# Scores and P times V tied in pairs in TensorE's order, from the ninth step of attention on

## The chip, the cores and the metric

The kernel runs on one core of a Trainium2 chip. The metric is the device time of one execution in microseconds, as a median of several runs.

## The reference

Attention over 2 batches, 8 heads, 768 positions and head size 64, with a local window of 96 positions, 8 global positions and a distance bias; then two feed-forward blocks on the 1536 resulting rows of 512.

```
scores = q @ k.T / sqrt(64) - slope[h] * dist     # masked to local or global positions
a      = softmax(scores)
x      = a @ v                                     # as 1536 rows x 512
h = x @ w_in;  x = (h * sigmoid(h)) @ w_out        # 512 -> 2048 -> 512
out = (sigmoid(x @ w_gate) * (x @ w_val)) @ w_out2 # 512 -> 1536 -> 512
```

## The kernel before

Attention works in units. A unit n is one block of 128 positions (`gi = n // 4`, 12 blocks over both batches) and one pair of heads (`p = n % 4`); there are 48. A unit goes through these stations: `emit_T` transposes the block's K and Q of two heads on TensorE into one PSUM bank (L339), and ScalarE or VectorE copies them out (L352, L350); `emit_QK` makes the scores against at most two blocks of keys (L376), with 64 contraction rows for each of the two heads; `soft` adds the mask, takes the maximum and later the exponent and the norm (VectorE L391, ScalarE L398, VectorE L404 and L405, GpSimd L407); `emit_PT` transposes the probabilities (L424), ScalarE copies them out to one of three `pt` buffers (L428); `emit_PV` multiplies with V (L445), 64 output columns for each head. After the fourth unit of a block, `take` copies the block's result to X and starts V loads on SyncE's queue (L462, L463). The scores of units n and n+1 go to two halves of the same two banks, one bank for each head of a pair.

A step of attention handles two units, n and n+1. Its first part, `head(n)`, emits P times V of n-4 and n-3, then scores of n and n+1, `take`, and both `soft`; then follow the transposes of probabilities of n-2 and n-1 and the transposes of K and Q of n+2 and n+3. The first six steps run alone (`run_att`). The steps from n = 12 on run in `window`, which mixes their parts with the first feed-forward block's matmuls for finished groups of 512 rows (L493: 512 columns, or 256 in the first items of `PLAN`). After the window `phase_rest` does the remaining feed-forward work. Weights are fetched and split into two parts by VectorE and ScalarE (L153 to L167) as the program goes on.

All instructions are emitted in one program order. A planner then makes each engine's own order from it: on each engine, what is ready goes first by program order, so that instructions that are neighbours in the program can end up far apart. On the chip each engine runs through its order as it stands.

Of the kernel before, what the change touches and what calls it, by code (L numbers as in the profile page):

```python
# [22 lines left out]
)  # L23
HA = 8
NEG = 1.0e30
LIMIT = 1.0e8
MAX_LOCAL = 121.0
# [4 lines left out]
def attn_moe_moe2_kernel(  # L32
# [88 lines left out]

    halves1 = [range(0, HA), range(HA, C1)]
    halves2 = [range(0, C2 // 2), range(C2 // 2, C2)]
# [131 lines left out]
    def make_mask0():  # L255
# [13 lines left out]
        nc.vector.tensor_tensor(gl, gl, loc[:, gs], ALU.add)  # L269
        nc.vector.tensor_scalar(gl, gl, -1.0, NEG, op0=ALU.add, op1=ALU.mult)  # L270
        nc.vector.tensor_scalar(loc, loc, -1.0, NEG, op0=ALU.add, op1=ALU.mult)
        nc.vector.tensor_tensor(m, m, loc, ALU.add)
# [4 lines left out]
    def make_mask1():  # L277
# [14 lines left out]
        nc.gpsimd.tensor_tensor(loc[:, gs], loc[:, gs], gl, ALU.add)  # L292
        nc.gpsimd.tensor_scalar(loc, loc, -1.0, NEG, op0=ALU.add, op1=ALU.mult)
        nc.gpsimd.tensor_tensor(m, m, loc, ALU.add)
# [36 lines left out]
    def emit_T(n):  # L331
        gi, p = divmod(n, NP)
        if gi >= NBLK:
            return
        s = gi % 2
        src = qk_t[gi]
        ps = bk["T"][n % len(bk["T"])]
        for j in range(2):
            nc.tensor.transpose(  # L339
                ps[:, j * 128:(j + 1) * 128],  # L340
                src[:, j, 2 * p:2 * p + 2, :].rearrange("p h d -> p (h d)"),
                ident,
            )

        def evac():
            sc = 2.0 ** (p - 1)
            dst = kT[p][:, slice(0, 3, 2) if s == 0 else slice(1, 3), :]
            pv = ps[:, 0:256].rearrange("p (a b) -> p a b", a=2)
            if n % 2:
                nc.vector.tensor_scalar(dst, pv, sc, None, op0=ALU.mult)  # L350
            else:
                nc.scalar.activation(out=dst, in_=pv, func=AF.Copy, scale=sc)  # L352
            i = gi % BLK
            if i == 0:
                nc.gpsimd.tensor_copy(kg[p], kT[p][:, s, 0:N_GLOB])
            elif i >= 2:
                nc.gpsimd.tensor_copy(kT[p][:, 1 - s, 0:N_GLOB], kg[p])

        evac()
        if p == NP - 1:  # L360
            load_qk(gi + 2)

    def emit_QK(n):
        gi, p = divmod(n, NP)
        if gi >= NBLK:
            return
        s, i = gi % 2, gi % BLK
        kt = kT[p]
        u, m = n % 2, n // 2
        sp = [bk["SA"][m % len(bk["SA"])], bk["SB"][m % len(bk["SB"])]]  # L370
        w = 128 if i == 0 else 256
        sp = [x[:, u * 256:u * 256 + w] for x in sp]
        for e in range(2):
            r = slice(64 * e, 64 * e + 64)
            rhs = kt[r, s, :] if i == 0 else kt[r, 0:2, :].rearrange("p a b -> p (a b)")
            nc.tensor.matmul(sp[e], kt[r, 2, :], rhs, start=True, stop=True)  # L376
        return sp

    def soft(n, sp):
        if sp is None:  # L380
            return
        gi, p = divmod(n, NP)
        s, i = gi % 2, gi % BLK
        w = 128 if i == 0 else 256
        t = t_p.tile([128, 2, 256], F32, tag="t", name="t")
        t_t[n] = t
        c = 2.0 ** -(2 * p + 1)
        m0 = 0 if i == 0 else (128 if s == 0 else 256)
        ss = ssum[n % 4]
        for e in range(2):  # L390
            nc.vector.tensor_tensor_reduce(  # L391
                t[:, e, 0:w], sp[e], mask[e][:, m0:m0 + w], op0=ALU.add, op1=ALU.min,
                scale=-c, scalar=3.0e38, accum_out=nm_all[:, gi, 2 * p + e:2 * p + e + 1],
            )

        def exps():
            for e in range(2):
                nc.scalar.activation(  # L398
                    out=t[:, e, 0:w], in_=t[:, e, 0:w], func=AF.Exp, scale=-1.0,
                    bias=nm_all[:, gi, 2 * p + e:2 * p + e + 1], accum_out=ss[:, e:e + 1],  # L400
                )

        def norm():
            nc.vector.tensor_scalar(ss, ss, 1.0e-9, None, op0=ALU.add)  # L404
            nc.vector.reciprocal(ss, ss)  # L405
            for e in range(2):
                nc.gpsimd.tensor_scalar(  # L407
                    t[:, e, 0:w], t[:, e, 0:w], ss[:, e:e + 1], 1.0, op0=ALU.mult, op1=ALU.mult
                )

        defer(1 + n % 2, exps)
        defer(2 + n % 2, norm)

    def emit_PT(n):
        gi, p = divmod(n, NP)
        if n < 0 or gi >= NBLK:
            return
        i = gi % BLK
        nk = 1 if i == 0 else 2
        t = t_t.pop(n)  # L420
        ps = bk["PT"][n % len(bk["PT"])]
        for e in range(2):
            for c in range(nk):
                nc.tensor.transpose(  # L424
                    ps[:, (e * nk + c) * 128:(e * nk + c + 1) * 128], t[:, e, c * 128:(c + 1) * 128], ident
                )
        pt = pt_p.tile([128, 512], F32, tag="pt", name="pt")
        nc.scalar.activation(out=pt[:, 0:256 * nk], in_=ps[:, 0:256 * nk], func=AF.Copy)  # L428
        pt_t[n] = pt

    def emit_PV(n):
        gi, p = divmod(n, NP)
        if n < 0 or gi >= NBLK:
            return
        s, i = gi % 2, gi % BLK
        pt = pt_t.pop(n)
        ps = bk["PV"][gi % len(bk["PV"])]
        if i == 0:
            vs = [v_t[gi]]
        else:  # L440
            vs = [v_t[gi], v_t[gi - 1]] if s == 0 else [v_t[gi - 1], v_t[gi]]
        nk = len(vs)
        for c in range(nk):
            for e in range(2):
                nc.tensor.matmul(  # L445
                    ps[64 * e:64 * e + 64, p * 128:(p + 1) * 128],
                    vs[c][:, (2 * p + e) * D:(2 * p + e + 1) * D],
                    pt[:, (e * nk + c) * 128:(e * nk + c + 1) * 128],
                    start=(c == 0),
                    stop=(c == nk - 1),  # L450
                )

    def take(n):
        gi, p = divmod(n, NP)
        if n < 0 or gi >= NBLK or p < NP - 1:
            return
        i = gi % BLK
        ps = bk["PV"][gi % len(bk["PV"])]
        g, j = divmod(gi, BPG)
        xs = slice(j * 128, (j + 1) * 128)  # L460
        pv = ps.rearrange("p (a b) -> p a b", a=NP)
        nc.scalar.activation(out=X[g][:, 0, :, xs], in_=pv, func=AF.Copy)  # L462
        nc.vector.tensor_tensor(X[g][:, 1, :, xs], pv, X[g][:, 0, :, xs].bitcast(F32), ALU.subtract)  # L463
        if 0 < i < BLK - 1:
            nc.sync.dma_start(
                out=v_t[gi][0:N_GLOB, :].rearrange("p (h d) -> p h d", h=H),
                in_=v[gi // BLK, :, 0:N_GLOB, :].rearrange("h p d -> p h d"),
            )
        load_v(gi + 2)

    def att_units(m0, m1):
        def head(n):
            emit_PV(n - 4)
            emit_PV(n - 3)
            sp = [emit_QK(n), emit_QK(n + 1)]
            take(n - 3)
            soft(n, sp[0])
            soft(n + 1, sp[1])

        for m in range(m0, m1):  # L480
            n = 2 * m
            yield lambda n=n: head(n)
            yield lambda n=n: emit_PT(n - 2)
            yield lambda n=n: emit_T(n + 2)
            yield lambda n=n: emit_PT(n - 1)
            yield lambda n=n: emit_T(n + 3)
# [463 lines left out]
```

## Time and profile before

| | |
|---|---|
| median of 3 runs | 699.97 us (698.42 to 701.34) |
| the profiled execution | 700.66 us |
| its span | 698.9 us |
| TensorE busy | 683.5 us, 98% of the span |
| VectorE, ScalarE, GpSimd busy | 374.4, 278.7, 88.8 us |
| granted TensorE clock, mean | 0.99 |

The span is the time from the first to the last instruction that the profiler saw; the execution's own time has a little around it. Times in the rows are microseconds from the start of the span unless marked ns. A busy TensorE is not TensorE at its peak: consecutive matmuls overlap in the rows, so the distance from start to start tells what a stretch of matmuls costs.

### The profile page before, as it was taken

Reading aid. Unit: us, or ns where it says so; the run is one execution under the profiler, and the core shown is the slowest. Engines: PE = TensorE matmul, PEld = TensorE weight load, DVE = VectorE, ACT = ScalarE, POOL = GpSimd, SP = SyncE. Lnnn points to the kernel's source line nnn. Section 1 sums busy time; section 2 is a strip of 40 time slices with the busy share of each in tenths; the row PEclk is TensorE's granted clock in tenths of the full one; section 3 lists DMA queues with packets and bytes.
Section 4 is the critical chain, followed back from the end, with each engine's and each line's share of the span. In section 5 each row is a group of like instructions: output and inputs, shape, how many; then the busy total and the mean of one; then the engine's idle time right before and its main releaser. Section 6 shows DMA issues by size and latency. Waiting matters only on the chain.

```text
span 698.9 us, 9181 instructions
## 1 busy us (share of the span) xinstructions
PE 683.5 (98%) x3393; PEld 534.9 (77%) x3393; DVE 374.4 (54%) x861; ACT 278.7 (40%) x594; POOL 88.8 (13%) x174
## 2 busy tenths in 40 slices
PE   7899999999999999999999999999999999999995
PEld 4467886667777888888888888888888888888884
DVE  4699995544459999752389941311684211212212
ACT  3688865464446565432265521111352111111110
POOL 5355553333320000000000000000000000000000
PEclk9799999999999999999999999999999999999999
DMA  9466562120002554500025420000240000100101
GB/s 210 127 163 157 165 194 61 31 48 16 17 2 83 163 177 124 177 1 0 1 79 159 153 91 1 1 0 1 60 151 0 1 1 0 61 0 1 61 0 65
DMA packets 65300, 49.03 MB, mean 70 GB/s; under 512 B 39648, under 2 KB 60128, under 8 KB 65248
## 3 DMA queue, kind: packets, MB, share of 16 engines
q1 hardware_dynamic: 64032, 48.11, 24.0%
q8 instruction: 28, 0.46, 0.3%
q10 hardware_dynamic: 1216, 0.26, 0.2%
q14 instruction: 24, 0.20, 0.1%
HBM read 45.22 MB, written 3.15 MB: 69 GB/s over the span
## 4 chain that ended last, share of the span: by engine, by line
PE 92%; DVE 5%; ACT 1%; issue 1%; DMA 1%; POOL 0%; DVEq 0%; ACTq 0%; POOLq 0%
PE bank L493 54%; PE bank L672 14%; PE bank L670 13%; PE bank L376 4%; PE bank L445 3%; PE bank L424 3%; PE bank L339 1%; DVE t L391 1%; DMA nraw<-in_n_local_dram 1%; ACT t L398 1%; DVE w L167 1%; DVE u L158 0%; DVE u L155 0%; POOL t L407 0%; DVE u L154 0%
## 5 line engine op out<-in xcount | busy, mean ns | idle before, releaser
L493 PE MATMUL bank<-x,w 128*128 128x512 f32 (+1 forms) x1488 | 356.7, 389 | 0.0
L493 PEld LDWEIGHTS bank<-x,w 128*128 128x128 f32 x1488 | 272.7, 188 | 63.2 <-issue 2.5
L530 DVE TENSOR_TENSOR sg<-sg,bank 128x512 f32<-128x512 f32 x36 | 24.8, 688 | 167.7 <-PE bank L493 167.7
L672 PE MATMUL bank<-w,g 128*128 128x512 f32 x432 | 104.5, 390 | 0.0
L672 PEld LDWEIGHTS bank<-w,g 128*128 128x128 f32 x432 | 81.1, 188 | 17.8
L670 PE MATMUL bank<-g,w 128*128 128x512 f32 x384 | 92.9, 390 | 0.0
L670 PEld LDWEIGHTS bank<-g,w 128*128 128x128 f32 x384 | 72.1, 188 | 15.9
L527 ACT ACTIVATE sg<-bank 128x512 f32<-128x512 f32 x36 | 21.5, 598 | 120.1 <-PE bank L493 120.0
L531 ACT ACTIVATE g<-sg 128x512 fp32r<-128x512 f32 x36 | 22.8, 633 | 93.8 <-DVE sg L530 93.8
L407 POOL TENSOR_SCALAR t<-t,ssum 128x256 f32<-128x256 f32 (+1 forms) x96 | 52.8, 566 | 53.9 <-DVE ssum L405 44.6
L166 ACT ACTIVATE w<-u 128x512 fp32r<-128x512 f32 x68 | 42.5, 632 | 33.2 <-DVE u L158 16.1
L153 ACT ACTIVATE u<-stage 128x512 f32<-128x512 f32 x68 | 45.5, 674 | 24.4 <-DVE w L167 19.7
L493 PE MATMUL bank<-g,w 128*128 128x512 f32 (+1 forms) x240 | 53.3, 359 | 0.5 <-DVE acc L577 0.3
L167 DVE TENSOR_TENSOR w<-u,w 128x512 fp32r<-128x512 f32 x68 | 46.9, 696 | 12.0 <-ACT w L166 11.7
L398 ACT ACTIVATE t<-t,nm_all 128x256 f32<-128x256 f32 (+1 forms) x96 | 46.2, 486 | 10.6 <-DVE nm_all L391 10.4
L155 DVE SCALAR_TENSOR_TENSOR u<-stage,u 128x512 int32<-128x512 int32 x68 | 48.7, 721 | 0.6
L158 DVE SCALAR_TENSOR_TENSOR u<-stage,u 128x512 int32<-128x512 int32 x68 | 47.0, 696 | 0.3
L391 DVE CUSTOM_DVE_ANT_0 t<-bank,mask 128x256 f32<-128x256 f32 (+1 forms) x96 | 33.8, 396 | 22.7 <-PE bank L376 13.7
L493 PEld LDWEIGHTS bank<-g,w 128*128 128x128 f32 x240 | 38.0, 189 | 8.6 <-issue 1.2
L518 ACT ACTIVATE g<-sg 128x512 fp32r<-128x512 f32 x48 | 30.3, 632 | 18.6 <-DVE sg L517 10.7
L376 PE MATMUL bank<-kt 64*128 64x256 f32 (+1 forms) x192 | 36.2, 449 | 1.1 <-DVE kt L350 0.6
L517 DVE SCALAR_TENSOR_TENSOR sg<-sg,bank 128x512 f32<-128x512 f32 x32 | 21.9, 685 | 26.5 <-ACT sg L516 26.2
(89 smaller groups left out, 496.4 us busy)
## 6 DMA issues: line engine op xcount, KB each, us to landing
stage<-in_moe_w_out_dram SPq DMA_DIRECT2D x28, 512.0 KB, 4.0
stage<-in_moe_w_in_dram SPq DMA_DIRECT2D x16, 512.0 KB, 6.1
stage<-in_moe_w_gate_dram SPq DMA_DIRECT2D x12, 512.0 KB, 3.4
stage<-in_moe_w_val_dram SPq DMA_DIRECT2D x12, 512.0 KB, 4.1
v<-in_v_dram SPq DMA_DIRECT2D x12, 256.0 KB, 3.0
out_dram<-acc SPq DMA_DIRECT2D x12, 256.0 KB, 2.0
qk<-in_k_dram SPq DMA_DIRECT2D x11, 256.0 KB, 3.3
qk<-in_q_dram SPq DMA_DIRECT2D x11, 256.0 KB, 5.1
```

The source lines that it names most:

```text
L153: nc.scalar.activation(out=st, in_=hw.bitcast(F32), func=AF.Copy, scale=2.0 ** -112)
L155: nc.vector.scalar_tensor_tensor(out=ui, in0=lw, scalar=29, in1=ui, op0=ALU.logical_shift_right, op1=ALU.bitwise_or)
L158: nc.vector.scalar_tensor_tensor(out=ui, in0=hw, scalar=-2 ** 31, in1=ui, op0=ALU.bitwise_and, op1=ALU.bitwise_or)
L166: nc.scalar.activation(out=w[:, 0, :], in_=st, func=AF.Copy)
L167: nc.vector.tensor_tensor(w[:, 1, :], st, w[:, 0, :].bitcast(F32), ALU.subtract)
L376: nc.tensor.matmul(sp[e], kt[r, 2, :], rhs, start=True, stop=True)
L391: nc.vector.tensor_tensor_reduce(t[:, e, 0:w], sp[e], mask[e][:, m0:m0 + w], op0=ALU.add, op1=ALU.min, scale=-c, scalar=3.0e38, accum_out= ...
L398: nc.scalar.activation(out=t[:, e, 0:w], in_=t[:, e, 0:w], func=AF.Exp, scale=-1.0, bias=nm_all[:, gi, 2 * p + e:2 * p + e + 1], accum_out ...
L407: nc.gpsimd.tensor_scalar(t[:, e, 0:w], t[:, e, 0:w], ss[:, e:e + 1], 1.0, op0=ALU.mult, op1=ALU.mult)
L493: nc.tensor.matmul(ps, wl[(slice(None), a) + wsl], xl[(slice(None), b) + xsl], start=(first and j == 0), stop=(last and j == len(order) - 1),)
L670: nc.tensor.matmul(yb[d], w[:, a, sl], gt[:, b, :], start=st, stop=en)
L672: nc.tensor.matmul(yb[d], gt[:, a, sl], w[:, b, :], start=st, stop=en)
```

## The change

From n = 16 on (the ninth step), `head` emits TensorE's part inside a manual schedule of that engine, which keeps the emitted order of these instructions on TensorE. The order in it is new: scores first, then P times V, and in each pair the later unit before the earlier one. Before n = 16 everything stays as it was. No instruction is added or removed.

```
+TIE = 16
 ...
         def head(n):
-            emit_PV(n - 4)
-            emit_PV(n - 3)
-            sp = [emit_QK(n), emit_QK(n + 1)]
+            if n < TIE:
+                emit_PV(n - 4)
+                emit_PV(n - 3)
+                sp = [emit_QK(n), emit_QK(n + 1)]
+            else:
+                with tc.manual_schedule(engines={mybir.EngineType.PE}):
+                    sp = [emit_QK(n + 1), emit_QK(n)][::-1]
+                    emit_PV(n - 3)
+                    emit_PV(n - 4)
             take(n - 3)
             soft(n, sp[0])
             soft(n + 1, sp[1])
```

## Rows read from the trace of the kernel before

**Rows 1.** The page: busy time of each engine; the chain that ended last.
```profile
PE 683.5 (98%) x3393; PEld 534.9 (77%) x3393; DVE 374.4 (54%) x861; ACT 278.7 (40%) x594; POOL 88.8 (13%) x174
...
PE 92%; DVE 5%; ACT 1%; issue 1%; DMA 1%; POOL 0%; DVEq 0%; ACTq 0%; POOLq 0%
```

**Rows 2.** Busy time by stretches of 14 us: engines, clock, DMA share, GB/s.
```profile
56.00:70.00 14.00, 13.68 (x120) 10.49 (x118) 13.68 (x42) 11.52 (x31) 6.87 (x12) 1.00 0.59 156
...
84.00:98.00 14.00, 14.00 (x100) 11.68 (x100) 13.95 (x41) 11.05 (x28) 7.68 (x12) 1.00 0.54 152
...
126.00:140.00 14.00, 14.00 (x95) 9.46 (x95) 7.67 (x32) 7.28 (x24) 4.50 (x12) 1.00 0.18 39
```

**Rows 3.** TensorE's waits, 55.83 to 210.81: total, times, longest; first and last.
```profile
PE bank L376 <- DVE nm_all L391: 0.4, 1, 0.4
...
PE bank L493 <- DVE acc L579: 0.2, 1, 0.2
```

**Rows 4.** Timeline of TensorE, single units: start, length, engine, line, operation.
```profile
111.56 1.55 PE L493 MATMUL bank<-g,w 128*128 128x512 f32 x6
112.95 1.31 PE L493 MATMUL bank<-x,w 128*128 128x512 f32 x5
...
122.35 0.70 PE L376 MATMUL bank<-kt 64*128 64x256 f32 x4
122.98 1.67 PE L493 MATMUL bank<-g,w 128*128 128x512 f32 x6
124.58 0.70 PE L376 MATMUL bank<-kt 64*128 64x256 f32 x4
...
204.78 0.66 PE L445 MATMUL bank<-pt,v 128*64 128x128 f32 x8
205.37 0.66 PE L424 MATMUL bank<-ident,t 128*128 128x128 f32 x4
...
208.37 1.66 PE L493 MATMUL bank<-g,w 128*128 128x512 f32 x6
```

**Rows 5.** Timeline of TensorE: first scores of head 16 and last P·V.
```profile
57.07 0.70 PE L376 MATMUL bank<-kt 64*128 64x256 f32 x4
...
209.96 0.66 PE L445 MATMUL bank<-pt,v 128*64 128x128 f32 x8
```

**Rows 6.** Timeline of TensorE, where two units stand together.
```profile
63.47 1.09 PE L445 MATMUL bank<-pt,v 128*64 128x128 f32 x16
64.49 0.66 PE L424 MATMUL bank<-ident,t 128*128 128x128 f32 x4
...
179.31 0.66 PE L445 MATMUL bank<-pt,v 128*64 128x128 f32 x8
179.90 1.14 PE L376 MATMUL bank<-kt 64*128 64x256 f32 x8
180.96 0.44 PE L339 MATMUL bank<-ident,qk 128*128 128x128 f32 x2
```

**Rows 7.** Timeline of TensorE's weight loads behind a P·V; idle before in brackets.
```profile
125.95 0.42 PEld L424 LDWEIGHTS bank<-ident,t 128*128 128x128 f32 x4 [0.17 <-issue]
126.34 0.30 PEld L493 LDWEIGHTS bank<-g,w 128*128 128x128 f32 x2
```

**Rows 8.** Timeline of TensorE: scores of units 34 and 35.
```profile
128.15 0.70 PE L376 MATMUL bank<-kt 64*128 64x256 f32 x4
...
131.54 0.70 PE L376 MATMUL bank<-kt 64*128 64x256 f32 x4
```

**Rows 9.** Timeline of VectorE: the first that reads those scores.
```profile
132.27 0.43 DVE L391 CUSTOM_DVE_ANT_0 t<-bank,mask 128x256 f32<-128x256 f32 x1
```

**Rows 10.** Timeline of GpSimd: norm of units 36 and 37.
```profile
143.14 1.85 POOL L407 TENSOR_SCALAR t<-t,ssum 128x256 f32<-128x256 f32 x4 [0.17 <-ACT t L398]
```

**Rows 11.** Timeline of TensorE: transposes of the probabilities of units 36 and 37.
```profile
162.14 0.65 PE L424 MATMUL bank<-ident,t 128*128 128x128 f32 x4
...
167.75 0.60 PE L424 MATMUL bank<-ident,t 128*128 128x128 f32 x4
```

## Prediction

> **What bounds the kernel now.** I read the page first: TensorE is busy 98% of the span and carries 92% of the chain that ended last [rows 1]. Then the table by stretches: from 56 to 210 us, where attention runs between the first expert's matmuls, TensorE is busy in practically all of every 14 us at a granted clock of 1.00, and the other engines have room, except VectorE, busy 13.4 to 13.95 of 14 us up to 98 us and about half after it [rows 2]. Then who waited for whom on TensorE in that part: four waits, from 0.4 down to 0.2 us, 1.2 us in all [rows 3]. So the part costs what TensorE's own stream costs, in its fixed order. An engine that is "busy" all the time can still lose time between its instructions, and the timeline of TensorE shows where, if one takes start to start instead of busy time.
>
> Three forms of matmul alternate: scores (L376, 64 contraction rows, two heads side by side), P times V (L445, 64 output columns, two heads side by side), and everything that uses the full array (transposes, expert matmuls). Inside a form the stream is tight: six full matmuls of 512 columns take 111.56 to 112.95, 1.39 us [rows 4]. Between two scores the same six take 122.98 to 124.58, 1.60 us, and between two P·V 208.37 to 209.96, 1.59 us [rows 4, 5]. So the edges of one excursion into another form and back add about 0.21 us to the neighbours. The excursion itself is longer when it is short: one unit of scores holds TensorE 0.63 us (122.35 to 122.98), two units together 1.06 us (179.90 to 180.96), so 0.20 us go at the ends; one unit of P·V 0.59 us (204.78 to 205.37), two together 1.02 us (63.47 to 64.49), so 0.16 us [rows 4, 6]. The weight loads say why: coming from P·V, the first load of a transpose waits 0.17 us with no releaser ("issue"), while the change from transposes to expert matmuls, both full array, shows no such idle time [rows 7].
>
> Price of a change of form, then: scores (0.20 + 0.21) / 2 = 0.205 us, P·V (0.16 + 0.21) / 2 = 0.185 us. If the neighbours hid their edges only the inside would count, 0.08 to 0.10 us. I take 0.18 us, near the upper end, since the edges are plainly there in the rows. The Trainium skill ("TensorE: Matmul & The Clock Gate", section "Step-by-step: what each phase is for") speaks against any such price: the queue pulls a weight load ahead of running matmuls if it goes to the background buffer, which would make the changes free. The rows contradict that here, and the skill's page "TensorEngine Tiling (Array Packing)", section "Key Properties", which says that a change of tiling mode drains the engine, agrees with them.
>
> **The change part by part.** *Count of changes of form.* From the first scores of head 16 at 57.07 to the last P·V at 209.96 [rows 5] I counted the timeline's stretches: 24 of scores alone, 32 of P·V alone, 4 where P·V is followed directly by scores. That makes 24 × 2 + 32 × 2 + 4 × 3 = 124 changes of form. Though the program writes the two P·V and two scores of a step next to each other, they run apart because each goes when its own input is ready.
>
> *What the tie does.* Both pairs are emitted with the later unit first. Scores of n+1 need the later transpose, and when that is there, scores of n can follow at once; the same with P·V of n-3 and n-4. So each pair should run as one stretch. Scores are in 16 of the changed heads (n = 16 to 46), P·V in 18 (n = 16 to 50). If pairs run whole, but the two pairs of a head apart, 34 excursions remain, 68 changes: 56 fewer, 56 × 0.18 = 10.1 us. If scores and P·V also stand together, 16 × 3 + 2 × 2 = 52 remain: 72 × 0.18 = 13.0 us. I take the first: P·V of the older units comes several us after the scores of its head in today's order, because its input is a transpose, an evacuation and a buffer further on.
>
> *What breaks it.* The order within a group is tied, not its contiguity; other work that becomes ready can get in. I allow one pair in eight: 4 pairs × 2 changes × 0.18 = 1.5 us. Bounds: none (0) and every second pair (34 / 2 × 2 × 0.18 = 6.1 us).
>
> *What is delayed.* Scores of n wait for scores of n+1. Today VectorE doesn't use them earlier anyway: scores at 128.15 and 131.54, first read by L391 at 132.27, after the second, both being in one bank [rows 8, 9]. So 0; without that cover it would be some 3 us of latency per step, which still is not on TensorE's path. P·V of n-4 waits for everything ahead of it in the group; it frees one of three `pt` buffers, so ScalarE's evacuation L428 of unit n-1 comes later, and behind that L398 in ScalarE's queue. There is room: GpSimd has normalised units 36 and 37 by 144.99, and their transposes run at 162.14 and 167.75 [rows 10, 11]. `take` with its V loads in SyncE's queue stays behind the same two P·V; it moves with them, by less than one unit, 0.43 us [rows 4, 6], and no V load is waited for. Cost 0, at most one 0.4 us wait as in [rows 3].
>
> *What is late next.* Where TensorE gets faster, VectorE has to keep up. After 98 us it has half its time free. From 56 to 98 us it has about 1 us of idle in 42; I expect little loss, because much of its work there is splitting weights that are used many microseconds later. Bounds: 0, and the whole gain of that stretch beyond VectorE's idle time: some 5 of 18 heads, 5 × 0.56 - 1.0 = 1.8 us.
>
> *Sum.* 10.1 - 1.5 = 8.6 us. The profiled execution took 700.66 us (span 698.9 and 1.8 us around it), so 692.1 us; it lies 0.7 us above the median of 699.97, against which the forecast is 691.4 us.
>
> **The rivals.** (a) *All four stand together*: one excursion per head, 13.0 us, 687.0 us. For it: one bank order and older P·V inputs ready; against it: the distance between scores and P·V today. (b) *VectorE becomes the bound up to 98 us*: 8.6 - 1.8 = 6.8 us, 693.2 us. For it its 13.95 of 14 us [rows 2]; against it the deferrable splits. (c) *Order without contact*: the group keeps its order but expert matmuls and transposes run between its members; half the pairs or more are broken, the gain is 10.1 - 6.1 = 4.0 us or less, and an ordinary stall takes part of it: about 698 us. That the change doesn't do what it says lies here too. (d) *Slower, by stalls at the head of the group*: TensorE takes its queue in order, and the first member of each group now stands for the latest input of a pair. If on the chip that input is later than the order was planned for, TensorE stands there with the whole queue behind it. The price of one such wait is 0.4 us [rows 3]; at all 34 pairs 34 × 0.4 = 13.6 us against 10.1 us: 703.5 us, and more where waits are longer. It decides from 10.1 / 34 = 0.30 us per pair. Against it: only four waits in 155 us today, and inputs that lie ready for many us. (e) *Changes of form are free*, as by the skill's rule above: 700 us; the rows exclude it nearly.
>
> **How the numbers follow.** Forecast 0.45, (a) 0.15, (b) 0.12, (c) 0.15, (d) 0.11, (e) 0.02. A measurement of this kernel tells about 0.5%, 3.5 us, from no change. Faster by more than that: forecast, (a), (b) and a corner of (c): 0.72; within: the rest of (c), (e) and a weak (d): 0.17; slower: 0.11. The range reaches from (a) with a little more for a higher price of a change, 72 × 0.185 = 13.3 us, 686.5 us, to (c) with some stalls, 700.5 us; only (d) is outside. Predicted time 691.4 us.
>
> **What would show it.** In the profile after: scores in stretches of eight matmuls and P·V in stretches of sixteen; about 70 changes of form instead of 124; the six expert matmuls at 1.39 us more often than at 1.60; the end of attention (last P·V, 209.96 now) some 8 to 9 us earlier, and the rest of the span unchanged in length. Wrong would be: stretches of four and eight still (c), waits ahead of L376 or L445 of 0.3 us and more at most heads (d), TensorE idle behind VectorE before 98 us (b).

## The result, and the profile after

The changed kernel takes 692.86 us (median; 692.11 to 694.6) against 699.79 us for the kernel before (six executions of each). The ratio is 0.9909, with a 95% interval of 0.9888 to 0.993: faster by 0.9%, or 6.9 us. The forecast was 691.4 us. An execution of one kernel can differ from the next by 3 us and more, so intervals are given throughout, and two kernels whose intervals overlap are told apart by stretches of their traces alone.

The profiled execution took 694.44 us, its span 692.6 us. From L25 on line numbers are higher by 1, and from the changed function on by 7: the expert matmuls of L493 are L500, P times V of L445 is L446, scores of L376 are L377, and the transposes (before L339 and L424) are L340 and L425.

The page's busy times, to be read beside [rows 1]: TensorE has lost 11.6 us of "busy" time, much more than the kernel got faster.

```profile
PE 671.9 (97%) x3393; PEld 533.3 (77%) x3393; DVE 371.4 (54%) x861; ACT 278.3 (40%) x594; POOL 89.2 (13%) x174
```

The timeline of TensorE (start, length, engine, line, operation, idle time before it) at head 16 and two later places. Scores now stand in eights and P times V in sixteens, where [rows 4, 5] have fours and eights.

```profile
54.97 0.38 PE L340 MATMUL bank<-ident,qk 128*128 128x128 f32 x2
55.11 1.55 PE L500 MATMUL bank<-g,w 128*128 128x256 f32 x11
...
57.77 1.14 PE L377 MATMUL bank<-kt 64*128 64x256 f32 x8
58.83 0.44 PE L340 MATMUL bank<-ident,qk 128*128 128x128 f32 x2
...
60.54 0.60 PE L425 MATMUL bank<-ident,t 128*128 128x128 f32 x4
60.98 0.38 PE L340 MATMUL bank<-ident,qk 128*128 128x128 f32 x2
63.38 1.09 PE L446 MATMUL bank<-pt,v 128*64 128x128 f32 x16 [2.03 <-ACT pt L429]
...
110.33 1.64 PE L500 MATMUL bank<-g,w 128*128 128x512 f32 x6
111.80 0.38 PE L425 MATMUL bank<-ident,t 128*128 128x128 f32 x2
112.02 0.38 PE L340 MATMUL bank<-ident,qk 128*128 128x128 f32 x2
112.74 1.66 PE L500 MATMUL bank<-g,w 128*128 128x512 f32 x6 [0.34 <-DVE acc L586]
...
201.11 1.09 PE L446 MATMUL bank<-pt,v 128*64 128x128 f32 x16
202.14 1.67 PE L500 MATMUL bank<-g,w 128*128 128x512 f32 x6
203.65 5.73 PE L500 MATMUL bank<-x,w 128*128 128x512 f32 x24
```

All 16 pairs of scores and all 18 pairs of P times V are whole (two of the pairs of P times V are eights: the four units of a batch's first block have half as many matmuls there). In TensorE's order 68 changes of form stand from the scores of unit 16 on; before there were 126 (the prediction counted 124). The weight loads that wait with no releaser show the same, over the whole kernel: first before, then after.

```profile
PEld bank L445 <- issue: 9.1, 37, 0.4
...
PEld bank L376 <- issue: 7.3, 29, 1.0
```

```profile
PEld bank L377 <- issue: 4.8, 18, 1.0
PEld bank L446 <- issue: 4.6, 17, 0.4
```

But TensorE now waits for others, where [rows 3] had 1.2 us in all. Who waited for whom on TensorE, from 54.97 to 203.7 us (total, times, longest):

```profile
PE bank L446 <- ACT pt L429: 2.3, 2, 2.0
PE bank L500 <- DVE acc L586: 1.4, 4, 0.3
PE bank L500 <- ACT x L463: 0.3, 1, 0.3
PE bank L377 <- DVE kt L351: 0.2, 1, 0.2
```

These idle times are too short, since the rows draw a matmul longer than its share of the stream: from 112.02, two transposes and the wait take 0.72 us until the next expert matmul, and the same two without a wait take 0.14 us (54.97 to 55.11), or 0.19 us after scores (139.67 to 139.86). So a wait shown as 0.34 costs 0.5 to 0.6 us.

**The account.** In both kernels TensorE runs the same matmuls in the same order up to the transposes of unit 17, at 56.76 us before and 54.97 us after, so this difference of 1.8 us isn't the change's. From there to the first matmul of the work after the window (212.32 before, 203.65 after) it is 155.56 us and 148.68 us, 6.88 us less. In the new order six expert matmuls of 512 columns fewer lie in that stretch and follow later, 6 × 0.232 = 1.39 us, so the true gain there is 5.5 us. From the 2000th matmul before the end to the last one both kernels take 461.6 us. What follows the last matmul was 1.0 us longer in this execution. So 1.8 + 5.5 - 1.0 = 6.3 us, the difference of the two spans. The medians of the two kernels differ by 6.9 us, with an interval of 4.9 to 7.8 us in which 5.5 lies: what goes beyond 5.5 us isn't traced to the change.

For all kernels I split the stretch from the 286th matmul (in P times V of unit 10) to the 2000th before the end into changes of form, waits (where the distance of two neighbouring matmuls from start to start exceeds what this pair of forms takes without a wait, the excess), and the rest. Changes are those of the whole stretch, so a few more than above.

| kernel | changes | stretch, us | waits, us | without waits, us |
|---|---|---|---|---|
| before | 127 | 173.8 | 1.5 | 172.3 |
| changed | 71 | 168.3 | 6.1 | 162.2 |
| changed, once more | 71 | 168.1 | 5.9 | 162.2 |
| scores tied only | 105 | 169.7 | 2.7 | 167.0 |
| P times V tied only | 97 | 170.6 | 2.9 | 167.7 |
| P times V ahead of scores | 55 | 168.5 | 8.8 | 159.6 |
| scores tied from 20 | 75 | 167.0 | 4.3 | 162.7 |
| changed, short addition | 71 | 165.6 | 3.2 | 162.4 |
| before, short addition | 128 | 174.3 | 1.2 | 173.1 |
| changed, evacuation first | 71 | 167.2 | 5.5 | 161.7 |

From before to after: 56 changes fewer, 10.1 us less without waits, 0.18 us for each change; and 4.6 us of new waits. The gain in the stretch, 5.5 us, is the difference of these two.

Not all of the 10.1 us is the price of a change, though. A unit's scores are one matmul for each of two heads (two in the rows), and the heads run side by side: in [rows 4] the four of one unit hold TensorE 0.63 us (122.35 to 122.98). In the kernel before three units stand with their two heads apart, and then the two matmuls of one head take the same 0.63 us (155.55 to 156.18); the other head's two stand with the next unit, and the six take 1.06 us, as long as eight in [rows 6]:

```profile
155.55 0.70 PE L376 MATMUL bank<-kt 64*128 64x256 f32 x2
156.18 0.66 PE L424 MATMUL bank<-ident,t 128*128 128x128 f32 x4
...
157.35 1.13 PE L376 MATMUL bank<-kt 64*128 64x256 f32 x6
158.41 0.44 PE L339 MATMUL bank<-ident,qk 128*128 128x128 f32 x2
```

From start to start the three units and a fourth (141.60), whose heads run side by side only in part, take 1.4 us longer than whole ones. In the changed kernel there are none of these. That leaves 8.7 us for 56 changes, 0.155 us each. The last column is no sharper than such things: the two kernels "before", one change apart, differ by 0.8 us in it, 0.5 us of it again by heads apart, and kernels with 71 changes by up to 0.7 us.

### The profile page after: what moved, and what is told of

It is laid out like the page before. It is cut to its first block, busy times and chain, and to the rows that moved or that the text cites. A ratio compares the mean times of both kernels' runs of the same rounds, so it can differ in the third digit from the quotient of the medians.

```text
span 692.6 us, 9158 instructions
## 1 busy us (share of the span) xinstructions
PE 671.9 (97%) x3393; PEld 533.3 (77%) x3393; DVE 371.4 (54%) x861; ACT 278.3 (40%) x594; POOL 89.2 (13%) x174
## 4 chain that ended last, share of the span: by engine, by line
PE 90%; DVE 6%; issue 1%; ACT 1%; DMA 1%; POOL 0%; DVEq 0%; ACTq 0%; POOLq 0%
PE bank L500 54%; PE bank L679 14%; PE bank L677 13%; PE bank L377 3%; PE bank L446 3%; PE bank L425 2%; DVE t L392 1%; PE bank L340 1%; DVE acc L586 1%; DVE u L159 1%; DVE u L156 1%; ACT t L399 1%; DMA nraw<-in_n_local_dram 1%; DVE w L168 0%; DVE u L155 0%
## 5 line engine op out<-in xcount | busy, mean ns | idle before, releaser
L500 PE MATMUL bank<-x,w 128*128 128x512 f32 (+1 forms) x1488 | 354.3, 388 | 0.3 <-ACT x L463 0.3
L500 PEld LDWEIGHTS bank<-x,w 128*128 128x128 f32 x1488 | 273.1, 188 | 62.6 <-issue 0.8
L534 ACT ACTIVATE sg<-bank 128x512 f32<-128x512 f32 x36 | 21.5, 597 | 120.2 <-PE bank L500 120.0
L500 PE MATMUL bank<-g,w 128*128 128x512 f32 (+1 forms) x240 | 54.1, 361 | 1.7 <-DVE acc L586 1.4
L167 ACT ACTIVATE w<-u 128x512 fp32r<-128x512 f32 x68 | 42.6, 630 | 26.9 <-PE bank L500 10.8
L392 DVE CUSTOM_DVE_ANT_0 t<-bank,mask 128x256 f32<-128x256 f32 (+1 forms) x96 | 33.7, 395 | 21.3 <-PE bank L377 15.1
L500 PEld LDWEIGHTS bank<-g,w 128*128 128x128 f32 x240 | 37.7, 189 | 8.8 <-DVE acc L586 3.5
L523 ACT ACTIVATE sg<-bank 128x512 f32<-128x512 f32 x32 | 19.0, 595 | 43.0 <-PE bank L500 42.7
```

What stands on the lines that cost most here:

```text
L167: nc.scalar.activation(out=w[:, 0, :], in_=st, func=AF.Copy)
L392: nc.vector.tensor_tensor_reduce(t[:, e, 0:w], sp[e], mask[e][:, m0:m0 + w], op0=ALU.add, op1=ALU.min, scale=-c, scalar=3.0e38, accum_out= ...
L500: nc.tensor.matmul(ps, wl[(slice(None), a) + wsl], xl[(slice(None), b) + xsl], start=(first and j == 0), stop=(last and j == len(order) - 1),)
```

## The experiments

The theories: **mine** is that each change of form costs about 0.18 us of TensorE's stream, whichever pair is tied, and that the waits are a separate bill with causes of its own. The rivals are that a change costs less and something else gained (or lost), or that the gain hangs on one of the two ties alone.

**Which part of the tie works.** This is seen in the planned orders alone, without a run. With scores first and the same tie, but the earlier unit first within each pair, the planner gives every engine exactly the order of the kernel before. With scores and P times V in two manual schedules instead of one, it gives exactly the order of the changed kernel. And with no manual schedule at all, each pair reversed and P times V still written ahead of scores, it gives exactly the order of the changed kernel too. So it is the reversed order in the pairs that gathers them, and the tie does nothing here: when the unit with the later input is first, its partner is as a rule ready the moment it may go.

**One tie alone.** Scores only:

```
+            emit_PV(n - 4)
+            emit_PV(n - 3)
             with tc.manual_schedule(engines={mybir.EngineType.PE}):
                 sp = [emit_QK(n + 1), emit_QK(n)][::-1]
-                emit_PV(n - 3)
-                emit_PV(n - 4)
```

> Only the scores are tied in pairs (later unit first) from step nine on; P times V stays free as before. In TensorE's order 102 changes of form stand from the scores of unit 16 on, against 126 before and 68 with both ties. Theory (each change costs about 0.18 us, waits are a separate account): 24 x 0.18 = 4.3 us below before, about 695.5 us, and no long wait ahead of the first tied P times V. Rival 1 (the price of a change is nearer 0.1 us and the rest of the gain came from something else): 2.4 us, about 697.4 us. Rival 2 (the gain hangs on P times V alone): no change, 699.8 us.

Measured 696.04 us against 699.2 us on that chip, ratio 0.9956 (0.9936 to 0.9975). Without waits the stretch is 5.3 us shorter than before for 22 changes, 0.24 us for each; less the 1.4 us of heads apart, which this tie mends as well, it is 3.9 us, 0.18 us for each. Against what I expected there is a long wait ahead of the first P times V of head 16, though that is not tied here; 1.3 us in the view of waits:

```profile
PE bank L446 <- ACT pt L429: 1.3, 1, 1.3
```

P times V only:

```
             with tc.manual_schedule(engines={mybir.EngineType.PE}):
-                sp = [emit_QK(n + 1), emit_QK(n)][::-1]
                 emit_PV(n - 3)
                 emit_PV(n - 4)
+            sp = [emit_QK(n), emit_QK(n + 1)]
```

> Only P times V is tied in pairs (later unit first) from step nine on; scores stay free. 96 changes of form against 126 before. Theory: 30 x 0.18 = 5.4 us below before, less the wait of about 2 us ahead of the first tied P times V if that wait belongs to this tie: 694.4 to 696.4 us. Rival 1 (0.1 us a change): 3.0 us less the wait: 696.8 to 698.8 us. Rival 2 (the gain hangs on the scores alone): 699.8 us or slower.

Measured 696.41 us against 699.2 us, 0.9952 (0.9932 to 0.9972). Without waits 4.6 us for 30 changes, 0.15 us for each (heads apart stay, 1.2 us of them), and no long wait for ScalarE's `pt`:

```profile
PE bank L500 <- DVE acc L586: 0.7, 2, 0.3
PE bank L340 <- ACT kt L353: 0.6, 2, 0.3
```

Together the two ties give 5.3 + 4.6 = 9.9 us without waits, and both at once gave 10.1: they add up. The rival that the gain hangs on one tie falls, since each kernel's interval lies below 1. Against a price of 0.1 us the whole times say little, as their intervals are nearly 3 us wide; the stretches without waits say 0.18 and 0.15 us.

**Fewer changes still.** P times V of the two units ahead of the two scores:

```
             with tc.manual_schedule(engines={mybir.EngineType.PE}):
-                sp = [emit_QK(n + 1), emit_QK(n)][::-1]
                 emit_PV(n - 3)
                 emit_PV(n - 4)
+                sp = [emit_QK(n + 1), emit_QK(n)][::-1]
```

> Both ties, but P times V of the two units ahead of the scores of the two units. 51 changes of form against 68 of the changed kernel. Theory: 17 x 0.18 = 3.1 us below the changed kernel, about 689.8 us, if no new waits come. Rival (waits grow as attention work is gathered in fewer places, because it no longer stands between the expert matmuls that share one bank): the 3.1 us are eaten by waits, 692.9 us or more, with more idle time of TensorE ahead of L500 behind VectorE's L586.

Measured 694.47 us against 699.2 us, 0.9931 (0.9909 to 0.9952). The price holds once more, 162.2 - 159.6 = 2.6 us for 16 changes, 0.16 us each, and 2.7 us of new waits eat it (stretch 168.5 us against 168.3). The rival had it right. From the view of waits:

```profile
PE bank L500 <- DVE acc L586: 2.2, 4, 1.2
PE bank L425 <- ACT pt L429: 1.7, 6, 0.4
```

**Whence the waits ahead of the expert matmuls.** Second matmuls of the feed-forward block (`y_part`) write one PSUM bank in turn; before the next six, VectorE must have added the bank to a running sum, 0.69 us. In the timeline above only the four transposes from 111.80 on lie between, less than 0.4 us of work, and the matmuls of 112.74 start when the addition is through:

```profile
112.00 0.69 DVE L586 TENSOR_TENSOR acc<-acc,bank 128x512 f32<-128x512 f32 x1 [0.30 <-PE bank L500]
```

Here the addition is shortened (cut down to the 512-column case):

```
-                nc.vector.tensor_tensor(a, a, yv, ALU.add)
+                nc.vector.tensor_tensor(a[:, 0:128], a[:, 0:128], yv[:, 0:128], ALU.add)
```

> The changed kernel, but in the window's 512-column items the addition of the second matmul's result to the running sum takes only 128 of 512 columns, so VectorE leaves the one shared bank earlier; three quarters of those additions are left out. Theory (TensorE's new waits ahead of L500 are the time in which this bank is emptied, since less attention work stands between): the waits ahead of L500 behind this addition, four of about 0.5 us with their hidden part and four of 0.2 to 0.3, go, and the time is 2 to 3 us below the changed kernel, 690 to 691 us. Rival (they come from the planner's order or from ScalarE): 692.9 us, waits as they were.

Measured 690.04 us against 699.2 us, 0.9884 (0.986 to 0.9909). The row `L500 <- DVE acc L586` is gone from the view of waits, and the waits fall by 2.9 us, the stretch by 2.7 us (165.6 against 168.3). The time is as the theory had it, but its interval overlaps that of the changed kernel (0.9888 to 0.993), so it is the stretch that tells the two apart. Its waits:

```profile
PE bank L446 <- ACT pt L429: 2.1, 2, 1.8
PE bank L500 <- ACT x L463: 0.3, 1, 0.3
PE bank L377 <- DVE kt L351: 0.2, 1, 0.2
```

The same shortening in the kernel before:

> The kernel before with the same shortened addition (128 of 512 columns in the window's 512-column items; three quarters of those additions are left out). Theory (before the change attention work stood between the expert matmuls that share a bank, so the addition was covered): only one wait of 0.26 us lay behind it, so at most 0.3 us, time as before. Rival (a shorter addition makes any order faster): 2 to 3 us below before.

Measured 698.84 us against 698.88 us, 1.0003 (0.9989 to 1.0018): no difference. So before the change the addition was covered, and after it no longer. That the cover were the attention units standing one by one between the expert matmuls is read from the timelines.

**Whence the long wait at head 16.** First a lighter VectorE:

```
-        nc.vector.scalar_tensor_tensor(
-            out=ui, in0=hw, scalar=-2 ** 31, in1=ui, op0=ALU.bitwise_and, op1=ALU.bitwise_or
-        )
```

> The changed kernel, with the last of VectorE's four steps in splitting a weight (the sign bits, about 0.7 us for each of 68 tiles) left out. Theory (the 2.1 us wait ahead of the first tied P times V is VectorE running behind up to 98 us: scores read late, exponents late, and the evacuation of the probabilities queued behind them on ScalarE): the waits before 80 us, 2.85 us together, shrink below 1 us, and the time is 2 to 3 us below the changed kernel, 690 to 691 us. Rival (the planner's order alone makes ScalarE late): the wait stays at about 2 us, 692.9 us.

Measured 696.21 us against 698.88 us, 0.9955 (0.9937 to 0.9972): not faster than the changed kernel, which took 693.5 us on that chip (below), and the waits before 70 us are longer (2.6 us for `pt` in two, 1.7 us for `kt` in one; the trace is of its fastest execution, 691.75 us). This settles nothing about VectorE's load: the planner moved later splits forward into the time set free, and VectorE was busy 13.80 of the 14 us from 56 to 70, as before.

Then the scores' tie from n = 20 only:

```
                 with tc.manual_schedule(engines={mybir.EngineType.PE}):
-                    sp = [emit_QK(n + 1), emit_QK(n)][::-1]
                     emit_PV(n - 3)
                     emit_PV(n - 4)
+                if n < 20:
+                    sp = [emit_QK(n), emit_QK(n + 1)]
+                else:
+                    with tc.manual_schedule(engines={mybir.EngineType.PE}):
+                        sp = [emit_QK(n + 1), emit_QK(n)][::-1]
```

> P times V tied from n = 16, scores tied from n = 20 only; 74 changes of form against 68. Theory (the long wait at 61 us belongs to the scores' tie, as it stands in the kernel with tied scores alone, 1.4 us, and not in that with tied P times V alone): no wait over 0.6 us before 80 us; 6 x 0.2 = 1.2 us more for changes, 2 us less wait, so about 692 us. Rival (the wait moves to the first tied scores, wherever they are): 693.5 to 694.5 us with a wait of over 1 us near 70 to 75 us.

Measured 692.55 us against 698.88 us, 0.9907 (0.9892 to 0.9922). The long wait is gone, no other of its length came in its place, and the stretch is 1.1 us shorter than that of the changed kernel, run beside it. Its waits:

```profile
PE bank L504 <- DVE acc L590: 1.4, 4, 0.3
PE bank L340 <- ACT kt L353: 0.3, 1, 0.3
PE bank L504 <- ACT x L463: 0.3, 1, 0.3
PE bank L446 <- ACT pt L429: 0.2, 1, 0.2
```

The changed kernel beside it:

> The changed kernel once more, on the same chip as the three others. Both theories: about 693 us, 6 to 8 us below before; the same twelve waits, 6 us in all, and 70 changes of form; only the stretch before 55 us may differ in length.

693.5 us against 698.88 us, 0.9929 (0.9908 to 0.9949), with the same twelve waits. The intervals of the two kernels overlap, so in whole times they are not told apart. The kernel with scores from 20 ran again on a third chip:

> P times V tied from n = 16 and scores from n = 20 once more, as a comparator on this chip: 692 to 693 us, 6 to 7 us below before, waits 4.3 us.

692.18 us against 698.04 us, 0.9915 (0.989 to 0.9941), waits 4.3 us as before.

Where the wait came from, ScalarE's timeline in the changed kernel shows:

```profile
60.11 0.37 ACT L353 ACTIVATE kt<-bank 128x256 f32<-128x256 f32 x1
61.24 0.63 ACT L167 ACTIVATE w<-u 128x512 fp32r<-128x512 f32 x1 [0.76 <-DVE u L159]
61.77 0.49 ACT L399 ACTIVATE t<-t,nm_all 128x256 f32<-128x256 f32 x1
...
62.27 0.49 ACT L399 ACTIVATE t<-t,nm_all 128x256 f32<-128x256 f32 x1
...
62.76 0.57 ACT L429 ACTIVATE pt<-bank 128x512 f32<-128x512 f32 x1
63.23 0.50 ACT L399 ACTIVATE t<-t,nm_all 128x256 f32<-128x256 f32 x1
```

The evacuation L429 of unit 13, for which P times V waits, could start when its transposes are through (they start at 60.54). It stands behind a weight copy L167, which waits for VectorE, and behind two exponents of units 16 and 17. With an ordering edge on ScalarE the exponents come after it (shortened; `ev[13]` is the evacuation of unit 13):

```
                 ex = nc.scalar.activation(out=t[:, e, 0:w], ... func=AF.Exp ...)
+                if n in (16, 17):
+                    tc.add_manual_dep(ex.ins, ev[13].ins.name, NoSync)     # after the evacuation of 13
```

> The changed kernel; in ScalarE's order alone, the evacuation of the probabilities of unit 13 stands ahead of the exponents of units 16 and 17, behind which it stood. 68 changes of form as before. Theory (the 2.1 us wait ahead of the first tied P times V is this place in ScalarE's order: the exponents wait there for scores that VectorE reads late): the wait falls below 0.7 us, the time by 1.3 to 2 us, to 691 to 691.5 us. Rival (VectorE's backlog as such, or the transposes, make the evacuation late): wait and time as in the changed kernel, 692.9 to 693.5 us.

Measured 690.39 us against 698.04 us, 0.9892 (0.9871 to 0.9913), the fastest kernel here that does all of the work, though its interval overlaps that of the changed one. By the ratios it is 1.2 us faster than that, and its stretch is 1.1 us shorter; the raw medians, 2.5 us apart, stand beside different runs of the kernel before (699.79 and 698.04 us). TensorE's order is that of the changed kernel up to 74.53 us of its trace. The wait falls from 2.1 to 1.1 us, by the two exponents; I had expected less than 0.7. The other waits grow by 0.4 us.

```profile
59.64 0.55 PE L457 MATMUL bank<-pt,v 128*64 128x128 f32 x6 [1.06 <-ACT pt L440]
```

ScalarE's timeline says what is left: the weight copy, still ahead and still late behind VectorE.

```profile
58.47 0.63 ACT L167 ACTIVATE w<-u 128x512 fp32r<-128x512 f32 x1 [0.76 <-DVE u L159]
59.00 0.58 ACT L440 ACTIVATE pt<-bank 128x512 f32<-128x512 f32 x1
59.48 0.50 ACT L404 ACTIVATE t<-t,nm_all 128x256 f32<-128x256 f32 x1
```

So half of the wait is shown to be a place in ScalarE's queue; that VectorE's backlog makes up the other half is read from these rows and was not separately shown.

**Both remedies at once.** The addition is shared, 288 columns on VectorE, 224 copied out by ScalarE and added by GpSimd:

```
+                tmp = ysp[d % 2]
+                nc.vector.tensor_tensor(a[:, 0:288], a[:, 0:288], yv[:, 0:288], ALU.add)
+                nc.scalar.activation(out=tmp, in_=yv[:, 288:512], func=AF.Copy)
+                nc.gpsimd.tensor_tensor(a[:, 288:512], a[:, 288:512], tmp, ALU.add)
```

> The changed kernel with the evacuation order of the run before and, in the window's 512-column items, the addition shared: VectorE adds 288 columns from the bank, ScalarE copies the other 224 out, GpSimd adds them. 67 changes of form. Theory (waits behind the bank are the time in which one engine empties it): four waits of 0.5 fall to about 0.2, those of 0.3 go, together 1.5 to 2 us, and with the other remedy 3 to 4 us below the changed kernel, 689 to 690.5 us. Rival (ScalarE's and VectorE's orders make one half late, so the bank is free no earlier): 691 us or more, waits ahead of L500 unchanged in sum.

Measured 692.96 us against 698.04 us, 0.9924 (0.9899 to 0.9949). A miss: the waits behind the addition are gone, but waits for ScalarE's `pt` and for VectorE ahead of the scores came instead, and the waits sum to 7.1 us by the split above.

```profile
PE bank L458 <- ACT pt L441: 3.4, 5, 1.1
PE bank L383 <- DVE ssum L417: 1.5, 3, 0.6
```

## Why the prediction was right, and where it wasn't

The direction and the main mechanism came out, and the time lies inside the range (691.4 forecast, 692.86 measured, 686.5 to 700.5). The gain that was forecast, 8.6 us, did not: where the change acts it is 5.5 us. Point by point:

- **The price of a change of form** was the step that carried the sum, 56 × 0.18 = 10.1 us; measured without waits 10.1 us for 56 changes. That the two agree is luck: 1.4 us of the 10.1 are heads of a unit that stood apart, which I counted as ordinary stretches, and the other 8.7 us are 0.155 us for each change. Scores cost 0.18 us and P times V 0.15 us, where I had 0.205 and 0.185. Too dear was what I put down to the neighbours: 0.21 us was read between expert matmuls of 512 columns, while all 61 stretches of full-array matmuls in the kernel before, start to start and without the waits, lose 0.16 us on average.
- **How the pairs stand** was right: pairs whole, scores and P times V of a head apart, so rival (a) did not come.
- **What breaks the pairs** was wrong: I took 1.5 us off for broken pairs, and none broke. That is no rule: with both remedies the scores of one pair did come apart (117.20 and 119.01 in that trace).
- **What is delayed: cost 0, at most one 0.4 us wait** was the step that failed most. New waits cost 4.6 us. About half of them, 2.1 us, is one wait: I had seen that ScalarE's evacuation stands in a queue with exponents, but only asked whether it is early enough on average ([rows 10, 11] are from a later part with much room), not at the first changed head, where VectorE is full. The other part, 2.9 us (0.3 of it stood there before), lies at a place that I didn't look at: I named who waits for the moved units, and not whom they had been covering. That scores of n wait for scores of n+1 cost nothing, as said: VectorE's L392 follows both scores (127.00 to 128.07) at once, at 128.17, as in [rows 8, 9].
- **VectorE up to 98 us**, rival (b), came at most in part, as the half of that wait which was not separately shown; not as a general slowing, since the following heads lose 0.2 to 0.3 us.
- **Rival (d)**, stalls at the head of the group, came at few groups: only 2.5 us of the waits shown stand at the head of a group (L446 and L377), and even all 4.6 us are 0.14 us for each of 34 pairs, below the 0.30 us from which it decides.
- **What would show it**: the eights and sixteens, about 70 changes (68) and the last P times V 8 to 9 us earlier (209.96 to 201.11) came as said. But the last of these flatters: 1.8 us of it was there before the first changed head, and 1.4 us are the six expert matmuls that follow later. The six expert matmuls at 1.39 us did not come more often: 13 such stretches take 1.46 or 1.47 us (110.33 to 111.80), 8 take 1.59 or 1.60, and none takes 1.39 (four did before).
- **The chances**: 0.72 for clearly faster is the forecast, (a) and (b) alone; the corner of (c) that is named with them adds nothing to it.

So the sum of 8.6 us lies near the measured 6.9 us partly by luck. Against the 5.5 us of the stretch it lacks 4.6 us of waits and takes off 1.5 us for broken pairs that stayed whole; the price of a change was 1.4 us too high over 56 changes, and heads apart, which were in no term, gave as much back.

## What to carry to other kernels

Where an engine is busy all the time, take start to start in its timeline and look for what alternates: on TensorE, matmuls with a part of the rows or columns of the array cost 0.15 to 0.18 us here at each change to another form, and gathering them pays it less often. A planner that runs what is ready scatters neighbours whose inputs come at different times; put the one with the latest input first, and the others follow it; here that needed no tie. And before work is gathered, ask what it was covering where it stood: here 2.9 of 10.1 us went to a PSUM bank that was emptied in its shade, and 2.1 us to one place in another engine's queue.

## What the runs showed of the hardware that I had not expected

- A unit's scores take as long with one head as with both: two matmuls 0.63 us, four 0.63 us. A planner that pulls the heads apart pays for it, 0.2 us and more for each unit besides the further changes of form.
- Executions of the same order differ most before head 16. TensorE's first 290 matmuls have the same order in all of these kernels but the one with the lighter VectorE. The 286th started at 56.1 us (before), 54.3 and 54.9 (changed, twice), 51.5 (evacuation first), 54.5 and 57.1 us (scores from 20, twice). Granted clocks go with a part of it: from 30 to 42 us 0.71 in the kernel before, 0.91 and 1.00 in the two of the changed kernel, 0.72 in the slowest start. In the kernel before TensorE was busy 7.81 us from 20 to 30 us, and from 30 to 36 us its clock stood at the lower of its two levels (0.50, 1.2 GHz). The rest isn't the clock: with 1.00 from 10 to 42 us, one start took 54.9 (changed, second time) and one 51.5 us. I leave its cause open; it is about as large as what several of these kernels differ by, so that stretches of the trace had to tell them apart, not whole times. The kernel before, from 20 us (columns as in [rows 2]):

```profile
20.00:30.00 10.00, 7.81 (x39) 4.27 (x38) 7.34 (x29) 7.04 (x21) 0.99 (x5) 0.83 0.49 124
30.00:36.00 6.00, 5.93 (x23) 2.83 (x24) 3.54 (x12) 3.12 (x8) 5.38 (x10) 0.50 0.47 148
```
